# Distances and identity by outer products on the matrix engine, head-pair loads of the first batch, and a crossbar turn of the attention output

## The chip, the core and the metric

The kernel runs on one core of one Trainium2 chip. The core has a matrix engine (TensorE, PE in the profile), a vector engine (VectorE, DVE), a scalar engine (ScalarE, ACT), GpSimd (POOL), a queue engine (SyncE, SP) and 16 DMA engines. The metric is device time in microseconds (us); less is better. One run was also profiled, and all durations below are from that one.

## The reference

Local attention with eight global keys feeds a gated long convolution. There are 4 batches, 8 heads, 768 positions and 64 values per head; heads side by side make 512 channels.

```python
scores = q @ k^T / 8                      # per batch and head, 768 x 768
rel = i - j;  keep = (j < 8) | (0 <= rel < 96)
dist = where((j < 8) & not local, 96, |rel|)
a = softmax(where(keep, scores - 2**-(h+1) * dist, -1e9))
x = (a @ v) with heads side by side       # (4, 768, 512)
x1, x2, x3 = split(x @ w_proj)            # 512 channels each
y = x1 * irfft(rfft(x2, axis=1) * rfft(filter_fft, axis=0)) * x3
out = y @ w_out
```

## The kernel before

**Plan and order.** The kernel does not leave the order to a scheduler. Python code first makes a graph of about 1000 operations, each with a planned cost and the data that it reads and writes. A constant string, `ORDER`, then lists them one by one: the number of the operation, the engine that takes it (P, A, V, G or S) and, for the matrix engine, the accumulation banks. `97P1 98V` is operation 97 on PE into bank 1 and operation 98 on VectorE. Where an operation may run on ACT or on DVE (evacuations of a bank), the string chooses. Words such as `i6b1` are six filler matmuls that compute nothing. Each engine and each DMA queue works through its own part strictly in that order, so a late operand holds up all that stands behind it on the same engine.

**Attention.** Keys are cut into seven tiles. Tiles 0 to 5 start at multiples of 120; each has 8 rows for the global keys and 120 local keys. A key tile meets at most 216 query columns. Queries and keys come from HBM with positions on the partitions (`qn`, `kn`, cast to 16 bits by GpSimd's DMA queue, L322) and must be turned so that the 64 head values lie on the partitions (`QT`, `KT`). Batches 0 to 2 are turned by PE (`turned`, L652; batch 0's queries, loaded in 32 bits by SP's queue, by `turned32`, L639) and the turned bank is evacuated by ACT or DVE (L306). Batch 3 is turned by DMA transposes on SP's queue (`crossed`, L626 and L629). The three groups of key tiles (0 and 1; 2 and 3; 4 to 6) are the chunks. `scores` (L693) multiplies one pair of heads for one chunk: two heads of 64 rows each use the two halves of the array. ACT takes the exponential (L707), DVE multiplies with `mask` (L724), which holds exp(-slope * distance). For batch 0 the mask is not yet there, and PE adds the bias instead: slopes on a diagonal (`slope`) times distances (`near`), L684.

**Distances.** `distances` makes the distance tables on GpSimd (an iota and affine selects, L484 to L504), DVE patches the global rows, and six copies on ACT and DVE spread them into `near`. The identity comes from GpSimd too; 16 small scalings on ACT (L310, `eo<-ident`) make `slope`.

**Values and the turn of x.** `values` (L742, L747) multiplies the exponentials with `vn`; a column of ones gives the sum. DVE takes the reciprocal (L771) and one multiplication (L766, or several on ACT, L770) writes `xn`, with positions on the partitions. `transpose_x` turns it on PE (L787), and ACT or DVE evacuate the bank into `xT` (L306).

**Convolution.** From `xT` come the gates x1 and x3 (`gate`, L856, evacuated at L310 and L866, multiplied at L868), and through `butterfly` (DVE, L801 to L812) the operands of x2's projection (L925), the forward transform (L613), the product with the filter's spectrum, the inverse transform (L950, L953) and `half` (L1051). Product with the gates (L1056) and output projection (L977) end the batch; each 128 positions are stored by one DMA on SP's queue (L985).

Attention of batch b+1 is interleaved with the convolution of batch b.

Of the kernel before, what the change touches and what calls it, by code (L numbers as in the profile page):

```python
# [9 lines left out]
F32 = mybir.dt.float32  # L10
# [6 lines left out]
P = 128  # L17
NG = 8
KL = P - NG
HUGE = 1.0e5  # L20
MAGIC = 12582912.0
# [18 lines left out]
0V 42V 3V 7V 27S 59S 28S 60S 61S 26S 69S 4G 54A 48A 45A 56A 50A 5V 1V 6V 29G 30G 66G 33G 65G 77G i6b1 17P0 18A  # L40
58A 47A 46A 43A 19V 11V 12P1 13A 49A 44A 57A 2A 14V 8V 15V 16A 55A 53A 20V 34V 39A 21A 51A 52A 22A 36A 37A 10V
40V 35G 70G 71G 72G 32G 68G 67G 73G i15b3 120P2 121V 9V 41V 93P3 94A 97P1 98V 82V 38V 258G 31G 74G 75G 267G
266G 226P0 95P4 96A 99A 230A 100P5 i1b6 122P2 123A 87A i1b1 126P3 127V 231V 269G i2b1 124P4 125V 101V 62V 64V
229V 268G 257G 255G 256G 259G 79G 76G 78G 80G 81G 262G i2b1 128P67 129A 134P23 135A 91P1 92V 24V 63V 132P45
133A 130P67 131A 102P23 103A 168P1 169V 227V 106P45 107A 170P6 171V 232V 166P7 167A 172P1 173V 228V 25V 261S
260S 263S 264S 275G 274G 273G 272G 265G 104P23 105A 108P45 109A 176P67 177A 178P01 179A 86A 136P23 137V 138V
141P45 142V 143V 174P67 175A 83A 115P23 116V 117V 110P01 111V 112V 180P45 181A 139P6 140A 89A 88A 144P7 145V
182P23 183V 184V 118P0 119A 85A 113P1 114V 187P45 188V 189V 383P7 185P6 186A 84A 384A 385P2 386V 213V 152P3
190P4 191V 212V 219V 215V 220V 357P6 147P2 149A 358A 154A 355P5 356V 198P4 200A 90A 359P2 360V 222V 214V 488G
271G 270G 496G 487G 489S 484G 495G 485G 193P7 195A 162P3 164A 396P01 397A 398V 216V 221V 364P45 361P67 362A  # L50
365A 208P2 210A 151P3 153V 366V 223V 23V 224V 225V 217V 146P0 148A 161P1 163A 165V 150V 218V 157P4 159A 370P67
393P23 394A 395V 367P01 368A 371A 192P5 194V 369V 372V 196V 156P4 158A 160V 155V 363V 233V 234V 235V 236V 237V
238V 239V 297P2 295P3 296A 387P01 388A 298A 390P67 280P4 281A 293P3 294A 391A 207P0 299P1 308P2 309A 300A
306P3 307A 301P5 203P4 205A 302A 284P2 285A 431P1 429P3 430A 432A 202P4 204V 209V 433P5 434A 490S 504G 486G
277G 503G 501G 276G 278G 506G 502G 494G 498G 378P67 379V 380V 392V 389V 252P23 253A 254A 240P4 241V 244P1 245A
246P5 247A 248P67 250A 249A 242P0 243A 373P23 374V 375V 206V 211V 719G 282P1 435P45 436A 283A 399P67 400V 401V
251V 441P23 442A 197P0 199A 404P45 405V 310V 406V 722G 491G 493S 720S 492S 381P1 382V 376P6 377A 288P7 289A
402P2 403V 443V 286P0 287A 583P3 407P4 408A 585P5 586V 437V 290V 584V 291V 303V 438P67 439A 440V 304V 292V
444P01 587P2 588A 445A 446V 311V 715G 717S 716G 409P4 419P5 410P6 412A 421A 420P7 595P23 596A 422A 598P01 599A
425P6 424P5 426A 427A 411A 447P23 448V 305V 449V 611P7 612A 723G 497G 279G 452P01 453V 454V 728G 505G 714G  # L60
500G 659P6 660A 324P5 314P4 315A 320P7 321V 428V 600V 312P2 316P3 317A 325A 313A 450P6 661P4 662A 318P0 455P3
456V 423V 201V 451V 478V 477V 413V 597V 479V 326P5 327A 319A 322P7 415P1 417A 323A 589P23 592P45 593A 811S
414P6 416A 468P0 470A 590A 458P1 460A 613P7 614V 418V 480V 328V 329V 481V 482V 594V 330V 483V 331V 591V 332V
457P6 459A 657P0 658A 729G 507G 734G 713G 712G 499G 730G 726G 727G 725G 732G 731G 724G 735G 733G 473P2 475A
618P45 619A 620V 333V 335V 621P67 615P01 616A 622A 463P3 472P2 474A 462P4 464A 465A 512P5 513A 521P6 522A
669P01 670A 624P23 625A 626V 525P7 526A 523P6 524A 672P45 663P01 664A 508P2 509A 673A 601P67 602V 334V 603V
623V 336V 665V 617V 671V 510P3 511A 467P0 536P1 537A 666P45 667A 668V 838S 718S 814S 813S 812S 837S 882S 721S
839S 883S 340P2 341A 469A 514P1 516P3 517A 515A 632P67 604P2 534P0 535A 538V 633V 674V 527P4 528A 605A 343P3
344A 606P01 607V 634V 608V 518V 352P5 353A 354S 529P4 530A 675P23 676V 519V 471V 635P5 636A 677A 627P67 609P4
610V 680P01 681V 628V 629V 532V 682V 531V 539V 520V 533V 346P5 337P4 338A 347A 339S 345S 342S 348S 349P6 630P7  # L70
631A 821P23 824P01 825A 350A 822A 351S 678P4 679V 826V 683P5 638P7 640A 684A 705V 653P0 548P6 546P1 547A 549A
550P2 544P3 554P7 555A 551A 545A 552P4 553V 706V 708V 707V 466V 461V 709V 476V 542P1 543A 655A 686P5 688A
691P4 693A 643P2 645A 540P3 541A 556V 843P67 840P01 841A 849P45 850A 647P2 649V 637P3 639A 844A 652P0 654V
823V 557V 558V 710V 559V 842V 560V 641V 711V 701P1 703A 893P45 846P23 847A 894A 815P67 736P0 737A 816A 817V
648P1 650A 749P2 890P45 891A 750A 696P3 698A 762P0 763A 832P67 833V 563V 651V 834V 561V 848V 892V 564V 753P1
754A 642P4 644A 751P5 752A 887P23 888A 884P01 818P67 819A 820V 845V 851V 895V 656V 740P4 741A 764P5 738P2 739A
885A 765A 766V 695P3 697A 700P4 742P2 743A 827P67 828V 829V 889V 886V 562V 757P0 758A 580P5 581A 702A 744P1
685P0 687A 755P5 756A 830P4 831A 745A 857P23 858V 859A 896P67 897V 898V 901P45 902V 903A 746V 747V 760V 689V
568P0 565P1 852P67 853V 854V 759V 748V 767V 571P2 572A 577P3 578A 860P4 690P5 861V 761V 835P2 836A 566A 855P3
856A 904P6 905A 899P7 900V 927V 926V 646V 929V 928V 930V 931V 704V 932V 574P2 575A 576S 567S 573S 582S 768P1  # L80
782P4 770P6 771A 569A 570S 579S 774P3 780P2 778P7 779A 783A 769A 868P6 776P0 777A 775A 772P7 773A 781A 784V
785V 786V 699V 787V 788V 791V 862P4 950P1 951A 933P7 934A 692A 694V 789V 792V 937P0 948P1 949A 938A 946P5
935P7 936A 947A 954P1 955A 867P0 952P3 959P5 961P7 962A 869A 953A 960A 872P1 874V 957V 956V 958V 963V 964V
941P2 942A 864A 870A 917P7 939P0 940A 943V 944V 945V 802P1 803A 805P5 878P6 863P4 865A 877P0 980P1 981V 866V
790V 971P4 972A 919A 879A 880A 808P3 984P4 978P2 982P7 983A 979A 967P1 968V 985V 986V 965P0 966A 969P6 970A
973V 881V 974V 975V 987V 976V 988V 977V 1004V 989V 799P7 793P4 794A 800A 801S 795S 804S 873P6 875A 809A 876V
871V 916P2 918A 796P1 797A 991V 990V 992V 993V 994V 920V 1006V 798S 810S 921P4 912P0 914A 911P3 913A 806A 923A
807S 922P2 906P1 908A 924A 925V 915V 907P3 909A 910V 1007V 1005V 1001P0 1002A 1003S 995P1 996A 997S 998P2 999A
1000S 1008P0 1009V 1010S 1014P1 1015V 1016S 1011P3 1012A 1013S
# [108 lines left out]
class Fused:  # L198
# [11 lines left out]
    CROSS = (3,)  # L210
    LATER = ()
# [8 lines left out]
    def __init__(self, ctx, tc, q, k, v, n_global, n_local, w_proj, filt, w_out, out):  # L220
# [10 lines left out]
        self.K0 = [KL * t for t in range(6)] + [S - KL]  # L231
# [6 lines left out]
    def buffers(self):  # L238
# [5 lines left out]
        self.qn = t("qn", [P, 6, H, D])  # L244
        self.kn = t("kn", [P, 7, H, D])
        self.vn = [t(f"vn{i}", [P, 7, H, self.VD]) for i in range(2)]
        self.QT = t("QT", [P, 4, S])
# [4 lines left out]
        self.xn = [t(f"xn{i}", [P, 2, 7, 2, D]) for i in range(2)]  # L252
# [12 lines left out]
        self.h1 = t("h1", [P, 6, DM])  # L265
        self.h2 = t("h2", [P, 6, DM])
# [14 lines left out]
        self.dg = t("dg", [P, 264], BF16)  # L281
        self.far = t("far", [NG, 216])
# [7 lines left out]
        self.row = spare[0:1, 1984:2624].rearrange("p (a b) -> p a b", a=5)  # L290
        self.wide_dg = self.mix.bitcast(BF16).rearrange("p a b c -> p (a b c)")[:, 0:648]
        self.cst = t("cst", [1, 4])
        self.one = t("one", [1, P])
# [31 lines left out]
    def load_rows(self, what, dst, src, b, t):  # L325

        lo, hi = self.K0[t], self.K0[t] + KL
        self.load("G", dst[P - (hi - lo):P, t, :, 0:self.D],
                  src[b, :, lo:hi, :].rearrange("h p d -> p h d"), [what + (t,)], (8 * (hi - lo), 256),
                  f"load{what}{t}")  # L330

    def load_run(self, what, dst, src, t, n):

        rows = src[0, :, self.K0[t]:self.K0[t] + KL * n, :].rearrange("h (t p) d -> p t h d", t=n)
        self.load("G", dst[NG:P, t:t + n, :, 0:self.D], rows, [what + (i,) for i in range(t, t + n)],
                  (8 * KL * n, 256), f"load{what}{t}")

    def load_q(self, b, t):
        src = self.q[b, :, P * t:P * t + P, :].rearrange("h p d -> p h d")
        if b == 0:  # L340
            st = self.ot[t].rearrange("p (h d) -> p h d", h=self.H)
            self.load("S", st, src, [("ot", t)], (1024, 256), f"q{t}")
            if self.Q32:
                return
# [896 lines left out]
```

## Time and profile before

| what | value |
|---|---|
| median of 3 runs | 173.8 us (173.58 to 174.24) |
| the profiled execution | 173.44 us, of it a span of 171.7 us from first to last instruction |
| granted matrix clock | 0.998 |
| busy share | PE 95%, DVE 91%, ACT 88%, POOL 45% |
| HBM read and written | 25.84 MB and 6.29 MB |
| queries of batch 3 stand turned (chain of work) | 99.96 us into the span |

The page gives the busy share of each engine, then the span in 40 slices with the busy share in tenths, then the chain of work that ended last and the groups of like instructions. A group's line has the source line, engine, operation, what it writes and reads, the shape, how often, the busy time, the mean of one in ns, and the idle time ahead of it with what ended it. Matmuls are pipelined: the mean of one is its latency, and the pace is read from the chain, where pieces stand end to end.

### The profile page before, as it was taken

To read this page: it belongs to the slowest core of one execution; us is meant where nothing else is said; L and a number is where in the kernel's file an instruction comes from. 1 tells how busy PE (TensorE), PEld (TensorE's weight loads), DVE (VectorE), ACT (ScalarE), POOL (GpSimd) and SP (SyncE) were. 2 spreads that over 40 slices of the span, in tenths; PEclk is the share of its full clock that TensorE was granted. 3 is DMA by queue.
4 is the path that set the end of the run, shared out by engine and by line. 5 is a ranking of instruction groups with operands and counts; after the bars stand their busy time and mean duration, and the time that the engine had idled before them with its cause. 6 is when DMAs were issued, how large, how long until landed. Compare 5 with 4: busy or idle time off the path is not lost.

```text
span 171.7 us, 4390 instructions
## 1 busy us (share of the span) xinstructions
PE 162.3 (95%) x1675; PEld 102.2 (60%) x1675; DVE 156.7 (91%) x355; ACT 151.1 (88%) x309; POOL 77.4 (45%) x95
## 2 busy tenths in 40 slices
PE   6888899999999979999999999999999999999990
PEld 1365689865464757965455767654576745575540
DVE  7997989989999899999999998999989999999960
ACT  5799999999899979999999999999998986866841
POOL 8999999962499994948993000000000000000000
PEclk9999999999999999999999999999999999999999
DMA  6999999999999999999999996500000360000854
GB/s 127 181 207 151 144 154 146 169 203 187 148 151 142 144 144 135 87 140 137 156 151 134 153 188 199 230 4 0 0 4 0 117 256 0 0 0 28 308 217 186
DMA packets 98077, 22.44 MB, mean 131 GB/s; under 512 B 90808, under 2 KB 94984, under 8 KB 98056
## 3 DMA queue, kind: packets, MB, share of 16 engines
q0 software_dynamic: 80912, 12.14, 100.3%
q1 hardware_dynamic: 17144, 10.02, 22.2%
q8 instruction: 13, 0.21, 0.5%
q14 instruction: 8, 0.07, 0.1%
HBM read 25.84 MB, written 6.29 MB: 187 GB/s over the span
## 4 chain that ended last, share of the span: by engine, by line
PE 72%; DMA 6%; POOL 6%; DVE 6%; ACT 6%; issue 2%; ACTq 0%; DVEq 0%
PE bank L856 23%; PE bank L925 9%; PE bank L977 9%; PE bank L950 5%; PE bank L693 5%; PE bank L613 5%; PE bank L652 4%; DMA QT<-qn 3%; PE bank L787 3%; PE bank L742 3%; DMA qn<-in_q_dram 3%; POOL kn L322 3%; PE bank L747 3%; POOL vn L322 2%; PE bank L684 2%
## 5 line engine op out<-in xcount | busy, mean ns | idle before, releaser
L856 PE MATMUL bank<-xT,w 128*128 128x384 f16 x256 | 47.4, 326 | 0.0
L707 ACT ACTIVATE E<-bank 128x864 f16<-128x864 f32 x48 | 41.4, 917 | 0.7 <-ACT h L310 0.3
L856 PEld LDWEIGHTS <-w 128*128 128x128 f16 x256 | 23.8, 98 | 16.3 <-issue 1.1
L322 POOL DMA_DIRECT2D vn<-in_v_dram x28 | 25.7, 923 | 4.4 <-DMA g<-in_moe_filter_fft_dram 3.9
L322 POOL DMA_DIRECT2D kn<-in_k_dram x28 | 25.9, 934 | 2.7 <-PE bank L856 2.2
L977 PE MATMUL bank<-wo,y 128*128 128x512 f16 x96 | 22.8, 379 | 0.0
L724 DVE TENSOR_TENSOR E<-E,mask 128x864 f16<-128x864 f16 x36 | 20.8, 603 | 0.8 <-ACT E L707 0.8
L322 POOL DMA_DIRECT2D qn<-in_q_dram x18 | 16.3, 917 | 6.1 <-PE bank L652 5.6
L310 ACT ACTIVATE ot<-bank 128x512 f32<-128x512 f32 x22 | 13.3, 618 | 4.6 <-PE bank L977 4.0
L866 ACT CAST g<-bank 128x384 f16<-128x384 f32 x32 | 15.9, 536 | 1.1 <-PE bank L856 0.9
L310 ACT ACTIVATE ab<-bank 128x512 f16<-128x512 f32 x24 | 14.2, 619 | 2.6 <-PE bank L925 2.5
L766 DVE TENSOR_TENSOR xn<-bank,rc 128x512 f16<-128x512 f32 (+1 forms) x21 | 16.0, 764 | 0.5
L742 PE MATMUL bank<-vn,E 128*128 128x65 f16 x224 | 15.3, 193 | 0.0
L742 PEld LDWEIGHTS <-E 128*128 128x128 f16 x224 | 14.0, 97 | 1.9
L747 PE MATMUL bank<-vn,E 128*128 128x65 f16 x192 | 15.1, 193 | 0.0
L977 PEld LDWEIGHTS <-y 128*128 128x128 f16 x96 | 8.9, 98 | 9.3 <-DVE y L1056 0.2
L693 PE MATMUL bank<-QT,KT 64*128 64x216 f16 (+2 forms) x224 | 13.9, 241 | 0.3 <-DMA QT<-qn 0.3
L306 ACT CAST X<-bank 128x512 f16<-128x512 f32 x24 | 13.6, 610 | 0.6 <-PE bank L613 0.5
L310 ACT ACTIVATE x<-bank 128x384 f16<-128x384 f32 x25 | 12.5, 526 | 1.3 <-DVE g L868 1.0
L747 PEld LDWEIGHTS <-E 128*128 128x128 f16 x192 | 13.2, 97 | 0.5
L306 ACT CAST eo<-bank 128x384 f16<-128x384 f32 x27 | 11.5, 508 | 1.4 <-PE bank L953 1.4
L693 PEld LDWEIGHTS <-KT 64*128 64x128 f16 x224 | 8.5, 94 | 6.3 <-issue 4.4
(142 smaller groups left out, 354.8 us busy)
## 6 DMA issues: line engine op xcount, KB each, us to landing
out_dram<-ot SPq DMA_DIRECT2D x24, 256.0 KB
kn<-in_k_dram POOLq DMA_DIRECT2D x28, 120.0 KB, 5.4
vn<-in_v_dram POOLq DMA_DIRECT2D x28, 120.0 KB, 5.2
qn<-in_q_dram POOLq DMA_DIRECT2D x18, 128.0 KB, 5.3
ot<-in_q_dram SPq DMA_DIRECT2D x6, 256.0 KB
w<-in_moe_w_proj_dram POOLq DMA_DIRECT2D x4, 256.0 KB, 6.7
g<-in_moe_filter_fft_dram POOLq DMA_DIRECT2D x1, 768.0 KB, 14.1
w<-in_moe_w_proj_dram POOLq DMA_DIRECT2D x1, 512.0 KB, 9.4
```

What stands on the lines that cost most here:

```text
L306: {"A": nc.scalar.copy, "V": nc.vector.tensor_copy, "G": nc.gpsimd.tensor_copy}[e](out, in_)
L310: self.nc.scalar.mul(out, in_, c)
L322: return self.g.op(eng, 0.57 + 0.00035 * nbytes[0] if eng == "G" else 0.5, lambda _: e.dma_start(dst, src), w=w, r=r, nbytes=nbytes, name= ...
L693: nc.tensor.matmul(bs[hh].f32()[:, off:off + w], self.KT[hs, m, hp], self.QT[hs, hp, KL * m:KL * m + w], start=(off == 0 and not near), st ...
L707: g.op("A", act(864), lambda _: nc.scalar.activation(eo, bs[0].two()[:, :, 0:432].rearrange("p h (m w) -> p h m w", m=2), Act.Exp, scale=s ...
L724: g.op("V", dve(864, 2), lambda _: nc.vector.tensor_mul(eo, eo, mk), r=[("mask", 2 * hp), ("mask", 2 * hp + 1)], w=[("E", hp, gi)], name=" ...
L742: nc.tensor.matmul(o[:, n, hh], ef[:, at:at + P], vt[:, t, 2 * hp + hh, 0:D + 1], start=first, stop=(t == 0), skip_group_check=True)
L747: nc.tensor.matmul(o[:, n, hh], ef[:, at:at + P], vt[:, t - 1, 2 * hp + hh, 0:D + 1], start=False, stop=True, skip_group_check=True)
L766: nc.vector.tensor_mul(to, o[:, :, :, 0:D], rc.to_broadcast([P, 2, 2 * nt, D]))
L856: nc.tensor.matmul(bk.f32()[:, 0:h], self.w[:, c, o + P * j:o + P * j + P], self.xT[:, c, h * s:h * s + h], start=(c == 0), stop=(c == 3))
L866: g.op("A", act(h), lambda _: nc.scalar.copy(x3, pts[1].f32()[:, 0:h]), use=[pts[1]], w=[ko], name="x3")
L977: nc.tensor.matmul(bk.f32(), y[:, c, P * t:P * t + P], self.wo[:, c, :], start=(c == 0), stop=(c == 3))
```

## The change

1. **Distances and identity** are made on PE by outer products of counting rows (`dist`), then turned into tables by two absolute values on ACT and some small DVE instructions. GpSimd makes no table any more. Eight slope scalings replace 16, and any may run on DVE.
2. **Batch 0** loads q and k per head pair, in token order (positions (6 x 128) instead of overlapping tiles), by eight DMAs of 1536 rows on GpSimd's queue; SP loads no queries. PE turns each pair with 12 transposes of 64 columns (`six`), and one evacuation (a 720 and a 48 column copy) cuts the tiles.
3. **Queries of all batches** lie in seven tiles of 120 positions (before: six of 128), so `QT` has the layout of `KT`. A score matmul of 216 or 168 columns becomes two (120 and 96, or 120 and 48).
4. **Batch 3's** q and k are turned by two DMA transposes each (before: six and three).
5. **x of batches 1 to 3** is turned by 21 DMA transposes on SP's queue, one for each tile (`crossed_x`), in place of `transpose_x` and its evacuation. `xn` is one tile with heads side by side, so a DVE scaling becomes two.
6. **The last 128 rows** of the output are projected, evacuated and stored in two halves of 256 columns.
7. Smaller memsets (only what is read of `vn`'s ones), a smaller h1/h2, and a new `ORDER` with 22 filler matmuls (before: 27).

```diff
@@ distances
-        def first(_):
-            for ap, w, base in ((dg[:, 0:n], n, NG), (dg[:, n:n + 48], 48, NG + o)):
-                p.iota(ap, pattern=[[-1, w]], base=-base, channel_multiplier=1,
...
+        def dist(_):
+            one, neg, n2, mm = self.one, self.neg, self.n2, nc.tensor.matmul
+            for k, bk in enumerate(bks):
+                o, w = bk.f32(), 384 if k == 0 else 264
+                mm(o[:, 0:w], neg, one[:, 0:1].to_broadcast([1, w]), start=True, stop=False, skip_group_check=True)
+                mm(o[:, 0:n], one, n2[:, NG:NG + n], start=False, stop=(k == 0), skip_group_check=True)
...
+                v.tensor_scalar(ident[lo:lo + 64, lo:lo + 64], d[lo:lo + 64], 0.0, None, op0=Alu.is_equal)
...
+                tt, bks[k].f32()[:, 0:w], Act.Abs, bias=self.mid, scale=HUGE2), use=[bks[k]], r=["mid", "ident"] if k == 0 else ["mid"],
...
@@ loads of batch 0
+    def load_six(self, what, dst, src, i):
+        self.load("G", dst[:, i], src[0, 2 * i:2 * i + 2].rearrange("h (t p) d -> p (h t) d", p=P),
+                  [(what + "six", i)], (1536, 256), f"six{what}{i}")
...
+    def six(self, what, i):
...
+            for r in range(6):
+                for hh in range(2):
+                    nc.tensor.transpose(b.f16()[64 * hh:64 * hh + 64, P * r:P * r + P], buf[:, r, hh], self.ident)
...
@@ scores
-                    nc.tensor.matmul(bs[hh].f32()[:, off:off + w],
-                                     self.KT[hs, m, hp],
-                                     self.QT[hs, hp, KL * m:KL * m + w],
...
+                for x in range(1 + (w > KL)):
+                    n = w - KL if x else min(w, KL)
+                    for hh in range(2):
+                        nc.tensor.matmul(bs[hh].f32()[:, off + KL * x:off + KL * x + n], self.KT[hs, m, hp],
+                                         self.QT[hs, m + x, hp, 0:n], start=(off == 0 and x == 0 and not near),
...
@@ the turn of x
+    def crossed_x(self, c):
+        for t in self.GRP[c]:
+            at, n = KL * t - 8 * (t % 2), (P if t % 2 else P - 16) if t < 6 else 48
+            self.g.op("S", 1.25, lambda _, at=at, n=n, t=t: self.nc.sync.dma_start(
+                self.xT[:, :, at:at + n], self.xn[0:n, t].rearrange("p h d -> p (h d)"), transpose=True),
...
             for j in range(2):
                 self.values(j, c, b % 2)
-                self.transpose_x(j, c)
+                if b not in self.XX:
+                    self.transpose_x(j, c)
+            if b in self.XX:
+                self.crossed_x(c)
...
@@ output
+            for lo, hi in ((0, 256), (256, 512)) if last and t == 5 and self.HALVES else ((0, 512),):
```

## The prediction

> **What bounds the kernel now.** I read the page's engine row and slices first, then three windows, then the chain.
>
> ```profile
> PE 162.3 (95%) x1675; PEld 102.2 (60%) x1675; DVE 156.7 (91%) x355; ACT 151.1 (88%) x309; POOL 77.4 (45%) x95
> DMA  6999999999999999999999996500000360000854
> PE 72%; DMA 6%; POOL 6%; DVE 6%; ACT 6%; issue 2%; ACTq 0%; DVEq 0%
> ```
> ```profile
> 0.00:20.00 20.00, 16.04 (x138) 9.34 (x139) 16.61 (x58) 16.97 (x41) 18.77 (x30) 1.00 1.60 163
> 20.00:160.00 140.00, 138.48 (x1501) 89.18 (x1500) 133.92 (x282) 128.36 (x258) 58.64 (x66) 1.00 1.23 119
> 160.00:171.70 11.70, 7.79 (x41) 3.72 (x38) 6.18 (x17) 5.73 (x13) 0.00 (x0) 0.98 0.57 219
> ```
> The columns of the windows are start:end, length, then PE, weight loads, DVE, ACT and POOL. From 20 to 160 us PE has work for 138.5 of 140 us: it is the bound, so a matmul less is time less. But DVE is close behind, idle for only 140 - 133.92 = 6.1 us; ACT has 11.6 us. In the first 20 us PE's 16 us hold much filler, and the chain runs over DVE and ACT:
>
> ```profile
> 3.88 0.84 DVE eo L385 x4
> 4.90 1.12 DVE kn L397
> 9.98 0.68 ACT eo L306 x2
> 13.42 0.96 ACT QT L306 x2
> 16.85 0.74 ACT mask L543
> 17.60 1.57 ACT E L707 x2
> 21.25 0.45 PE bank L639 x4
> 28.81 0.45 PE bank L787 x8
> 35.99 0.67 PE bank L693 x12
> 88.82 5.37 DMA qn<-in_q_dram
> 94.19 5.77 DMA QT<-qn
> 117.83 0.67 PE bank L693 x16
> ```
> The pace of PE is read here: 0.45/8 = 56 ns for a 16-bit turn (L787; L652 stands in the chain at the same 0.45 for 8), 112 ns for a 32-bit turn (L639). Batch 3's queries take 11 us from their issue to PE, through a load and a transpose.
>
> **PE, part by part.**
> *x turned elsewhere.* 112 turns become 28: 84 x 56 ns = -4.7 us, all on the path. PE's wait for `xn` ahead of them (1.0 us, row L787 below) loses its place too; I count it at nothing, since the next values wait for the same DVE.
> *Scores in two pieces.* 224 matmuls become 416. The two heads of a pair run side by side, and the columns stay the same. The two L693 rows show what pieces cost: 12 matmuls of 216 columns took 0.67 us, and 16 of mixed widths (216, 168, 48) with the same total of columns took 0.67 us too. Bounds: 0, and 0.03 us for each of 96 extra pairs (the pace of a 65 column values matmul, pieces of 0.06 for two in the chain) = 2.9 us. I take +0.4, near the row of the same instruction.
> *q and k of batches 1 and 2.* 48 query turns become 56: 8 x 56 ns = +0.45 us.
> *Batch 0.* 24 x 112 + 28 x 56 ns = 4.3 us go; 96 turns with half the columns of the array come. Bounds: 28 ns each if two lie side by side (2.7 us) and 56 ns if not (5.4 us). I take 35 ns, 3.4 us, because the score rows show halves side by side: -0.9 us (-1.6 to +1.1). The 8 distance matmuls (some 1560 columns, about 0.7 us) and 5 fillers less lie in the start, where PE waits anyway.
> After the start this leaves -4.7 + 0.4 + 0.45 = -3.9 us (-4.7 to -0.9).
>
> **ACT and DVE.**
> ```profile
> L787 PE MATMUL bank<-ident,xn 128*128 128x128 f16 x112 | 9.1, 219 | 1.0 <-DVE xn L766 1.0
> L306 ACT COPY xT<-bank 128x480 f16<-128x480 f16 x10 | 5.9, 585 | 2.1 <-PE bank L787 2.1
> L306 DVE COPY xT<-bank 128x480 f16<-128x480 f16 x6 | 2.3, 400 | 0.0
> L766 DVE TENSOR_TENSOR xn<-bank,rc 128x512 f16<-128x512 f32 x15 | 10.2, 687 | 0.3
> L310 ACT ACTIVATE eo<-ident 64x64 bf16<-64x64 f16 x16 | 3.4, 248 | 0.1
> ```
> ACT: 13 evacuations of xT become 3 (-8 x 0.585 - 2 x 0.696 = -6.1 us); 16 slope scalings and 6 table copies (3.4 + 2.3) give way to 5 scalings and 2 absolute values (about 2.2): -3.5; 12 more small xn scalings at 0.21 each +2.5; four more x1 evacuations +2.1; fewer of ab, X and ot -4; the rest +1.4. Sum -7.6 us.
> DVE: 11 evacuations of xT become 3 (-3.4); 21 xn scalings become 32 of about half the size (17 pieces replaced by 26 at 0.42 to 0.55): +0.8; x1 evacuations -2.2; ab, X and ot taken over from ACT +4.5; smaller memsets of vn and kn -3.4; tables and batch 0's evacuations about +2; the rest -0.5. Sum -2.2 us, of it some -0.7 ahead of the first reciprocal and -1.5 behind. So DVE gains least: if PE's 140 us shrink by 3.9, DVE has to do 132.4 us of work in 136.1, 97.3% instead of 95.7%. I give back 1.0 us for that (0 to 3).
>
> **The start.** The first exponential starts at 17.50 us. Ahead of it ACT loses 16 scalings (3.4), table copies (2.3), three QT casts (1.6), the twin, KT and inr copies (1.4) and a mask (0.7), 9.4 us; it gains two absolute values (0.9), three scalings (0.75), a copy of v's first rows (0.6), an evacuation each of k and q (2 x 1.0) and a small copy (0.2), 4.5 us: -4.9. DVE's counting row drops from seven dependent doublings (2.1 us) to two instructions. What may be late in its place is the load: POOL takes 0.92 us for 960 rows, so 1.47 for 1536 (an estimate); the third load, the first pair's second half, is issued by 0.7 + 3 x 1.47 = 5.1 us and lands 5.4 us later (page, kn), at 10.5. Turn, evacuation, sines (1.0) and a table load (1.3) put the first exponential at 14 to 14.6, some 3 us earlier. The last queries are the tenth load in the queue (issued by 14.3, landed by 20) and needed for the ninth exponential, at about 21. POOL pays 12288 rows instead of 6720, +5.3 us, and loses its table work (4.34 to 8.52 us and 0.6), so v, w and batch 1's loads behind them stand where they stood. I take -2.5 us (0 to -4.9); batch 0's PE gain lies in it.
>
> **The end.** The last evacuation shrinks from 0.60 to about 0.40: -0.2 us.
>
> **SP and DMA.** 21 turns at the measured issue of 1.5 us (row below) are 32 us of a queue that has the room. Behind them stand stores and the copies of global rows; ahead of batch 2's first turn stand batch 3's first KT and QT transposes, which wait for loads.
> ```profile
> L629 SPq DMA_TRANSPOSE QT<-qn x6: 1192/1515/2042, 88.9 to 103.5; - x6
> ```
> That is an answer on the tile QT: least, median and greatest ns of an issue. A chunk's last three turns take 3 x 1.5 + 5.8 = 10.3 us from `xn` to the butterfly. Between them the new order lays DVE work of about 9.3, 10.3 and 7.5 us (batches 1 to 3, products at 0.69, masks at 0.60, g at 0.35). Batch 3 is short by 2.8; but its transposes find no loads in the way, and the 5.8 was taken while loads ran, so I count nothing.
>
> The skill weighs against this part. The Trainium skill, VectorE: DVE Perf Modes, "The three transpose paths", gives a 128 x 128 turn 390 ns on TensorE and 1309 ns through the crossbar, and its rules for kernel authors send such turns to TensorE when PSUM will do. No row here times one block alone. By that figure, as an estimate, three tiles (12 blocks) would take 15.7 us, 20 us more than the three covers together, and the kernel would be near 188 us.
>
> **Sum.** -2.5 - 3.9 + 1.0 - 0.2 = -5.6 us on the profiled execution's 173.44, 167.9; that run lies 0.36 us under the median of 173.8. I forecast 168.0 us. Its own range, with the bounds above, is 165.5 to 170.
>
> **Rivals.**
> *DVE binds* (0.18). The idle share of DVE stays as it is and the new order has no better fit. Then only 1.5 us behind the start, 1 us in it and 0.2 at the end are won: 170.7 us. For: 95.7% busy. Against: in the windows from 140 to 160 us it already ran at 97%.
> *Turns late* (0.12). At the greatest issue, 3 x 2.04 + 5.77 = 11.9 us, the three covers are short by 2.6, 1.6 and 4.4; at the median by 1.0, 0 and 2.8. DVE stands at the butterfly, masks and reciprocals queue behind it, and PE follows. That takes 3.8 to 8.6 us off the gain; near the lower end 172.5.
> *Batch 3's loads late* (0.12), the slower side. The DMA row reads 9 until slice 24. The 14 turns of batches 1 and 2 add 7168 rows of 256 B; at the mean pace of small packets (90808 in 103 us, 880 per us) that is 8.1 us if there is no room. Batch 3's queries would stand turned at 100 - 2.5 + 8.1 = 105.6, and behind that point PE saves only 28 turns (1.6) and the end: 173.44 + 5.6 - 1.8 = 177.2 us. It decides from about 4 us of lateness on. Against: a DMA engine counts as busy while a packet is under way, POOL waits longest for buffers that PE holds (5.6 us, L652), and its waits from 36 to 81 us come to 12.8 us, over a quarter of that stretch.
> *All bounds good* (0.03): 163.5 us.
>
> **Chances.** Forecast 0.55. About 0.5% can be told from no change here. Faster: 0.55 + 0.18 + 0.03 and a third of the late turns, 0.80; same, most of the other late turns, 0.08; slower 0.12. The range leaves out the late loads and the outermost late turns above, and the best case below: 164 to 173.5.
>
> **What would show it.** Right: first exponential near 14 us; L787 with 28 turns and L693 with 416 at unchanged busy time for a chunk; DVE over 93% of a span of 166. Wrong: PE waiting for `DMA xT` or DVE waiting for `DMA xT` at the butterfly (late turns); a wait for `DMA QT` or `DMA KT` of several us before batch 3's scores (late loads); PE idle behind DVE in every stage (DVE binds); L693's pieces at over 30 ns a pair more (split not free).

## The result and the profile after

The changed kernel took 179.56 us (median of 4 runs, 178.28 to 181.23), the kernel before 173.69 beside it: 1.0346 times as long (95% interval 1.0291 to 1.0401). Forecast were 168.0 us and a range of 164.0 to 173.5. The profiled execution took 179.99 us with a span of 178.2. Medians below are over all runs, while ratios and their intervals leave out every run more than 1.5% above the fastest of its kernel (two of four in e4), so the two can differ by a per cent, and the profiles of e1, e4, e5, e10 and e17 are of runs left out.

The page of the changed kernel, in the rows that were shown of before:

```profile
PE 165.5 (93%) x1842; PEld 101.4 (57%) x1842; DVE 153.8 (86%) x383; ACT 145.0 (81%) x297; POOL 74.7 (42%) x89
...
DMA  6999999999999999999999999927103220404446
...
PE 67%; DMA 15%; DVE 7%; POOL 6%; issue 2%; SPq 1%; ACT 1%; DVEq 0%
```

DVE and ACT have less to do, as forecast (156.7 to 153.8 and 151.1 to 145.0 us). But the DMA share of the chain rose from 6% to 15%, and the DMA engines stay at 9 through slice 26 instead of 24. The windows (start:end, length, then PE, weight loads, DVE, ACT, POOL, granted clock, DMA share, GB/s):

```profile
0.00:20.00 20.00, 18.77 (x195) 9.65 (x197) 13.94 (x71) 11.88 (x25) 14.34 (x19) 1.00 1.63 105
20.00:160.00 140.00, 131.99 (x1559) 83.10 (x1555) 127.34 (x281) 121.82 (x250) 60.38 (x71) 0.99 1.38 129
160.00:178.20 18.20, 14.70 (x98) 8.61 (x94) 12.55 (x35) 11.27 (x24) 0.00 (x0) 0.98 0.49 187
```

From 20 to 160 us PE now lacks 8.0 us of work, 6.5 more than before. The chain, from three stretches, shows where (start, length, what):

```profile
7.96 1.82 PE bank L314 x4
9.78 0.78 PE bank L682 x10
10.55 1.39 PE bank L314 x3
...
64.43 6.63 DMA kn<-in_k_dram
71.10 0.62 PE bank L707 x8
...
99.35 8.73 DMA xT<-xn
108.08 0.05 issue
108.13 0.82 PE bank L930 x4
```

Three places answer to the forecast's steps. At the start the turns of batch 0 (L682) stand behind filler matmuls (L314). At 71 us PE takes up batch 2's keys as soon as their load lands, 6.6 us after its issue. At 108 us the first gate of batch 2 (L930) stands at a crossbar turn of x. PE's waits for DMAs in this kernel (total, times, longest):

```profile
PE bank L751 <- DMA QT<-qn: 2.9, 1, 2.9
...
PE bank L930 <- DMA xT<-xn: 2.2, 1, 2.2
...
PE bank L707 <- DMA kn<-in_k_dram: 0.7, 1, 0.7
```

The groups that the change meant to shrink did shrink (112 turns of x to 28, 24 evacuations to 6, three of them on ACT; the scalings of the three batches are smaller and more). Line, engine, what, count, busy, mean ns:

```profile
L832 DVE TENSOR_TENSOR xn<-bank,rc 128x256 f16<-128x256 f32 (+1 forms) x26 | 10.9, 464 | 0.1
...
L853 PE MATMUL bank<-ident,xn 128*128 128x128 f16 x28 | 2.0, 219 | 0.0
```

and the turns that take their place are, one by one, cheaper than priced. From the answer on the tile xT (least, median, greatest; ns of SP's queue for the issue, then us to landing):

```profile
L863 SPq DMA_TRANSPOSE xT<-xn x21: 1177/1262/2435, 58.8 to 139.2; - x21
...
DMA to landing us min/median/max: 2.3/5.1/8.3
```

Priced were 1.5 and 5.8. So the question was where 12 us went although the median turn was no dearer than its price.

### The profile page after: what moved, and what is told of

The parts are those of the page before. It is cut to its first block, busy times and chain, and to the rows that moved or that the text cites. A ratio compares the mean times of both kernels' runs of the same rounds, so it can differ in the third digit from the quotient of the medians.

```text
span 178.2 us, 4734 instructions
## 1 busy us (share of the span) xinstructions
PE 165.5 (93%) x1842; PEld 101.4 (57%) x1842; DVE 153.8 (86%) x383; ACT 145.0 (81%) x297; POOL 74.7 (42%) x89
## 4 chain that ended last, share of the span: by engine, by line
PE 67%; DMA 15%; DVE 7%; POOL 6%; issue 2%; SPq 1%; ACT 1%; DVEq 0%
PE bank L930 20%; PE bank L1065 11%; PE bank L1010 8%; DMA g<-in_moe_filter_fft_dram 6%; PE bank L314 5%; DMA xT<-xn 5%; PE bank L635 4%; PE bank L1035 4%; DMA kn<-in_k_dram 4%; PE bank L751 4%; PE bank L801 2%; POOL vn L334 2%; PE bank L707 2%; PE bank L806 2%; POOL kn L334 2%
## 5 line engine op out<-in xcount | busy, mean ns | idle before, releaser
L930 PE MATMUL bank<-xT,w 128*128 128x384 f16 x256 | 48.8, 332 | 3.1 <-DMA xT<-xn 2.2
L930 PEld LDWEIGHTS <-w 128*128 128x128 f16 x256 | 24.1, 99 | 20.5 <-DMA xT<-xn 2.7
L334 POOL DMA_DIRECT2D qn<-in_q_dram x25 | 23.0, 923 | 12.9 <-PE bank L707 6.9
L334 POOL DMA_DIRECT2D kn<-in_k_dram x25 | 22.5, 906 | 6.2 <-PE bank L682 3.1
L1065 PE MATMUL bank<-wo,y 128*128 128x512 f16 (+1 forms) x100 | 23.3, 371 | 0.0
L751 PE MATMUL bank<-QT,KT 64*128 64x120 f16 (+2 forms) x416 | 15.3, 204 | 3.4 <-DMA QT<-qn 2.9
L751 PEld LDWEIGHTS <-KT 64*128 64x128 f16 x416 | 11.3, 94 | 10.6 <-issue 8.4
L322 ACT ACTIVATE x<-bank 128x384 f16<-128x384 f32 x29 | 14.4, 525 | 0.7 <-PE bank L930 0.5
L801 PE MATMUL bank<-vn,E 128*128 128x65 f16 x224 | 14.8, 193 | 0.0
L322 ACT ACTIVATE ot<-bank 128x512 f32<-128x512 f32 (+1 forms) x20 | 12.1, 609 | 3.4 <-PE bank L1065 2.4
L806 PE MATMUL bank<-vn,E 128*128 128x65 f16 x192 | 14.6, 193 | 0.0
L635 PE MATMUL bank<-ab,fwd 128*128 128x512 f16 x40 | 11.8, 379 | 0.1
```

The costliest lines, as they stand in the source:

```text
L322: self.nc.scalar.mul(out, in_, c)
L334: return self.g.op(eng, 0.57 + 0.00035 * nbytes[0] if eng == "G" else 0.5, lambda _: e.dma_start(dst, src), w=w, r=r, nbytes=nbytes, name= ...
L635: self.nc.tensor.matmul(b.f32(), self.fwd[:, f], src(i, t), start=(n == 0), stop=(n == len(terms) - 1))
L751: nc.tensor.matmul(bs[hh].f32()[:, off + KL * x:off + KL * x + n], self.KT[hs, m, hp], self.QT[hs, m + x, hp, 0:n], start=(off == 0 and x ...
L801: nc.tensor.matmul(o[:, n, hh], ef[:, at:at + P], vt[:, t, 2 * hp + hh, 0:D + 1], start=first, stop=(t == 0), skip_group_check=True)
L806: nc.tensor.matmul(o[:, n, hh], ef[:, at:at + P], vt[:, t - 1, 2 * hp + hh, 0:D + 1], start=False, stop=True, skip_group_check=True)
```

## Experiments: turning x elsewhere, and the queue

Theories, in the names of the expectations: Q, batch 2's turns stand on SP's queue behind batch 3's transposes; C (later G), the turns slow what runs beside them; S, the start; P, the new order or batch 0's loads; T, the crossbar turns in whatever way; W, waits that other work could cover.

**Batch 3's transposes behind batch 2's turns.**
```diff
- ... 328S 691S 783S 785S 329P1 ...  654S 655S 653S 784S 786S
+ ... 328S 691S 329P1 ...            654S 655S 653S 783S 785S 784S 786S
```


> The changed kernel took 179.6 us, 11.6 more than forecast. Edit: on SP's queue the first KT and the first QT transpose of batch 3 are issued behind the last x turn of batch 2 instead of ahead of its first; nothing else moves. Theory Q (queue): batch 2's x turns stand behind these two (1.4 and 5.0 us of issue) and land late, which costs PE 5.1 us of waiting from 90 to 110 us and about 2 us by the clock that drops behind it; then batch 2's first gates start near 101 us instead of 108 and the time is 173 to 176 us. Theory C (contention): every crossbar turn slows all rows that the DMA engines move, whatever its order; then batch 3's queries and keys now come late instead, and the time is 178 to 182 us. Theory S (start): the loss is the missing gain at the start; 179 to 180 us.

188.23 us, 1.07 (1.0584 to 1.0815) against before. PE's first scores of batch 3 now wait:

```profile
PE bank L751 <- DMA QT<-qn: 11.2, 1, 11.2
```

All three expectations missed. The order of the queue was the better one already: with batch 3's transposes second PE stands 11.2 us at them, where it stood 2.9 us at them and 2.2 us at the turn before.

**x on PE for batch 2, and for all batches.**
```diff
-    XX = (1, 2, 3)
+    XX = (1, 3)          # e2;   XX = ()  in e3, each turn and evacuation behind its scaling in ORDER
```


> Edit: batch 2's x is turned on PE and evacuated as before the change; its seven crossbar turns go; batches 1 and 3 keep theirs. It costs PE 28 turns, 1.6 us, and ACT and DVE three evacuations each. Theory Q: the stall from 98 to 108 us and the clock drop go, 173 to 175 us. Theory C: a third of the turns go, and with them a third of the loss, 176 to 178 us. Theory S: 180 to 181 us.

> Edit: x of all batches is turned on PE, as before the change; no crossbar turn of x is left, the rest of the change stays. By the forecast's own prices this kernel should lose 4.7 us of PE's gain and keep the start's 2.5 and the end's 0.2, so 171.5 to 172.5 us. Theories Q and C: 171 to 174 us, since both put the loss on the turns. Theory S: the start brings nothing and the x turns cost nothing, so 179 to 184 us.

179.38 (ratio 1.0315) and 191.38 (1.0924): both misses, and neither is a price of the turn. PE stood at the scalings, which the turns on PE need first, 5.2 us in e2 (three waits ahead of L853) and longer in e3:

```profile
PE bank L853 <- ACT xn L836: 6.7, 3, 3.1
PE bank L853 <- DVE xn L826: 2.3, 4, 1.5
```

Two more such versions, with the turns further back, did not mend it.
```diff
-    XX = (1, 2, 3)
+    XX = (3,)            # turns 1.5 to 2.6 us of PE work behind the scalings (e7); scalings all on DVE (e12)
```


> Edit: x of batches 1 and 2 is turned on PE again, with each group of turns put behind 1.5 to 2.6 us of other PE work after its scaling, so that PE does not stand at it (the kernels that turned x on PE before this one put it right behind and lost several us there); batch 3's seven turns stay on the crossbar, where no loads run. PE gets 56 turns more, 3.1 us. Theory T: 172 to 175 us. Theory P: 179 to 182 us.

> A version that might win. Edit: x of batches 1 and 2 on PE (56 turns, 3.1 us), its scalings all on DVE (0.69 us in one instruction instead of up to 2.46 us in 12 on ACT, behind which PE stood in the last such kernel), the evacuations on ACT; batch 3's x on the crossbar. Theory T: no crossbar turn of x is left beside the loads, 171 to 175 us. If PE turns placed into this order still make PE wait, 176 to 181 us.

183.73 (1.0553) and 182.55 (1.0563). Both missed their ranges. PE still waits at single places, and query buffers are freed late; in e7 POOL's loads of queries show it:

```profile
POOL qn L334 <- PE bank L707: 15.9, 2, 13.1
```

These four show only that this order has no room for turns on PE; a new order for them was not made.

**The turns alone in the kernel before.**
```diff
-                self.transpose_x(j, c)
+            if b in self.XX:            # (1, 2, 3); before's ORDER, crossx behind the two scalings
+                self.crossed_x(c)
```


> The kernel before, in its own order, its own start and its own scores, with this one part of the change: x of batches 1 to 3 is turned by 21 crossbar DMAs, each issued on SP behind the two scalings that it needs; PE's 84 turns and 18 evacuations go, and the scalings of DVE come in two halves. Theory T: the turns cost more than PE's 4.7 us, 176 to 182 us. Theory P: PE gains without the new order's loss, 169 to 172 us.

211.25 us, 1.2074 (1.195 to 1.2198), far above both ranges. The gates of before's order follow the scalings closely, and PE stands at the turns in four waits (gate is L875 here):

```profile
PE bank L875 <- DMA xT<-xn: 31.1, 4, 10.4
```

The new order hides most of that: 2.2 us of waiting for `xT` are left in the changed kernel.

## Experiments: what of a turn costs the time

**8-row copies, and plain copies of the same bytes, at the turns' places.**
```diff
-                self.xT[:, :, at:at + n], self.xn[0:n, t].rearrange("p h d -> p (h d)"), transpose=True),
+                self.xT[0:8, 0, at:at + n], self.xn[0:8, t].rearrange("p h d -> p (h d)")[:, 0:n]),   # e5
+                self.xT[0:n, :, at:at + n], ...rearrange("p (a c) -> p a c", a=4)[:, :, 0:n]),        # e6
```


> Edit: each of the 21 crossbar turns of x becomes a plain copy of 8 rows of 96 to 256 B into xT, at the same place of SP's queue and with the same waits; the turning of x is left out, and nobody does it. So PE, DVE and ACT have the work of the changed kernel without the turns' issue time, landing and traffic. Theory T (the turns, by SP's issue time of 26 us between 86 and 115 us and by their landing): the stalls of PE near 70 to 80 and 90 to 110 us go, 168 to 172 us. Theory P (the new order, or batch 0's 128-byte loads): the turns are not what is late, 176 to 180 us.

> Edit: each of the 21 crossbar turns becomes a plain DMA of the same bytes (4 pieces of up to 256 B for each of up to 128 partitions), so x is copied and not turned. Theory T by the crossbar (issue and landing of a transposing DMA): a plain copy issues in 0.7 us instead of 1.2 to 2.5, the stalls shrink, and the time lies near that of the 8-row copies, 169 to 173 us. Theory T by traffic (7168 more rows in the stretch in which the loads run): the rows are still there, 176 to 180 us.

The 8-row copies gave 170.3 to 175.4 us in four runs, too wide for an interval, with a median of 174.64 between its two ranges. The plain copies gave 173.37 us in ten, 0.9992 (0.995 to 1.0035) of before, just above the range for the crossbar's theory and below that for the rows'. So 21 DMAs of the same bytes, with the same waits, at the same places, cost 6 us less than 21 transposing ones: it is the transposing, not the rows. The shorter issue on SP's queue comes with the plain copy and was not tried apart from it. The issue halves, the median landing hardly changes:

```profile
L863 SPq DMA_DIRECT2D xT<-xn x21: 607/655/2167, 56.0 to 131.0; - x21
...
DMA to landing us min/median/max: 2.3/4.8/9.8
```

**Only batch 2's, only batch 1's turns as plain copies.**
```diff
-            self.g.op("S", 1.25, lambda _, at=at, n=n, t=t: self.nc.sync.dma_start(
+            self.g.op("S", 1.25, lambda _, at=at, n=n, t=t, plain=self.b in (2,): ...   # the copy of e6 if plain; (1,) in e18
```


> Edit: only batch 2's seven turns of x become plain DMAs of the same bytes (batch 2's x is copied, not turned); batches 1 and 3 keep theirs. All three plain gave 173.4, none 179.6. Crowding (batch 2's turns, batch 3's transposes and loads together from 86 to 115 us): 4 to 6 us go, 173.5 to 175.5 us. Each turn alike: a third goes, 177 to 178.5 us.

> Edit: only batch 1's seven turns become plain DMAs (batch 1's x is copied, not turned). Crowding: only the stall near 70 to 80 us goes (batch 2's keys land 6.6 us after their issue there, PE idle 1.6), 177.5 to 179 us. Each turn alike: 177 to 178.5 us, and as much as batch 2's.

176.29 (1.0157, 1.0076 to 1.0238) and 176.72 (1.0204, 1.0124 to 1.0284): the first lies between its two ranges, the second just under both. Batch 2's turns cost 3.3 us and batch 1's 2.5 by the ratios (1.0346 less these, of 174), each uncertain by more than a microsecond; together they come near the 6. Batch 3's turns were not tried alone. The windows tell the two apart (PE is the second column after the times). First the changed kernel, then batch 2 plain, then batch 1 plain:

```profile
60.00:80.00 20.00, 17.91 (x268) 12.75 (x264) 17.95 (x42) 18.29 (x39) 13.35 (x16) 1.00 2.33 141
...
90.00:120.00 30.00, 24.90 (x263) 15.38 (x260) 22.48 (x53) 22.18 (x60) 5.83 (x7) 0.94 1.52 139
```
```profile
60.00:80.00 20.00, 17.47 (x268) 12.77 (x266) 17.51 (x42) 17.85 (x39) 12.78 (x15) 1.00 2.19 139
...
90.00:120.00 30.00, 26.85 (x300) 16.65 (x298) 24.72 (x57) 24.07 (x65) 6.33 (x8) 0.94 1.58 145
```
```profile
60.00:80.00 20.00, 19.46 (x287) 13.62 (x284) 19.58 (x46) 19.81 (x42) 14.98 (x18) 1.00 1.78 139
...
90.00:120.00 30.00, 24.45 (x255) 14.79 (x252) 22.44 (x50) 21.70 (x54) 3.36 (x4) 0.94 1.42 154
```

Batch 1's turns make PE's 2.1 us of idling from 60 to 80 us (0.5 without them), batch 2's make 2 us of the 5.1 from 90 to 120. The other kernels bear it out, whatever their start: from 60 to 80 us PE idles 1.9 to 3.2 us in the ten with batch 1's turns on the crossbar, 0.1 to 0.5 in the five with copies at their places (e5, e6, e9, e16, e18); from 90 to 120 us 4.6 to 11.3 us in nine with batch 2's turns, 1.3 to 3.2 in five with copies. The granted clock does not tell the three kernels apart (0.94 from 90 to 120 us in each).

What batch 2's turns do there is a plain wait: with them copied, PE's 2.2 us at `xT` are gone, and the wait for batch 3's queries, 2.9 us above, stays:

```profile
PE bank L751 <- DMA QT<-qn: 3.2, 1, 3.2
```

How batch 1's do it is in the DMA view of 56 to 76 us, the changed kernel first, then batch 1 plain (queue: packets, MB, time of the packets as a share of 16 engines; then a load with its median us to landing):

```profile
GB/s 151 162 158 165 145 150 151 151 158 226 199 57 42 104 146 154 155 170 155 143 152 217 152 114 147 222 43 11 51 141 150 144 155 149 155 141 152 149 151 152
...
q0 software_dynamic: 18551, 2.25, 217.3%
...
kn<-in_k_dram POOLq DMA_DIRECT2D x6, 120.0 KB, 6.4
```
```profile
GB/s 153 147 146 159 148 130 95 131 146 137 162 159 157 147 153 149 146 160 191 204 176 225 161 153 144 152 148 151 154 148 150 153 158 177 183 144 140 59 221 178
...
q0 software_dynamic: 18732, 2.22, 177.9%
...
kn<-in_k_dram POOLq DMA_DIRECT2D x6, 120.0 KB, 5.4
```

About as many load packets take 23% longer each (217.3% of 16 engines' 20 us for 18551 packets, 37.5 ns each, against 177.9% for 18732, 30.4 ns), and the median load of keys lands a microsecond later. PE meets that at 71 us. Every kernel of the new order says the same: from 56 to 76 us it is 33 to 45 ns in the ten with batch 1's turns on the crossbar, and 30.4 to 30.6 ns in the eight without (plain copies, 8-row copies or turns on PE). The traffic also falls to 42 and to 11 GB/s (slices of 0.5 us), the second time while the load of keys in the chain is under way; but single slices fall low without crossbar turns too (59 here, 26 in e6), so this alone shows nothing.

**Batch 3's q and k as plain copies, with and without x's.**
```diff
-            g.op("S", 1.25, lambda _, dst=dst, src=src: sync.dma_start(dst, src, transpose=True), ...
+            g.op("S", 1.25, lambda _, dst=dst, src=src: sync.dma_start(dst, src), ...   # src as 128-column blocks
```


> Edit: only the four transposes of batch 3's queries and keys become plain DMAs of the same bytes (q and k of batch 3 are not turned); the 21 turns of x stay on the crossbar. Theory Q (in line on SP: x's turns stand behind the merged transposes' 5.0 and 6.7 us of issue): the stall near 98 to 108 us goes, 172 to 175 us, near that of plain x turns. If the x turns' own landing is what is late, the stall stays: 177 to 180 us.

> Edit: besides the 21 turns of x, the four transposes of batch 3's queries and keys become plain DMAs of the same bytes too, at the same places; x of batches 1 to 3 and batch 3's q and k are copied and not turned, nobody turns them. With only the x turns plain the time was 173.4 us, and 12.0 us passed there between the issue of the three-tile QT transpose and its landing, with 2.9 us of PE waiting for it and a clock of 0.86 behind. Theory T, carried on: the rest of the forecast's gain is lost in this one transpose; without it 167.5 to 170 us. Rival (the new order or the loads take the rest): 172 to 174 us.

177.86 (1.0278) with x on the crossbar, 172.02 (0.9915, 0.9871 to 0.9958) with nothing on it. The second lies in its rival's range and not in theory T's: batch 3's transposes are not where most of the rest was lost. The first is what was expected if x's turns land late by themselves. Theory Q falls once more: with batch 3's transposes gone PE waits for x itself, 4.6 us instead of 2.2.

```profile
PE bank L930 <- DMA xT<-xn: 4.6, 1, 4.6
```

**Smaller transposes for batch 3.**
```diff
-    QX = ((0, 3), (3, 7));  KX = ((0, 2), (2, 7))
+    QX = ((0, 1), (1, 2), (2, 3), (3, 5), (5, 7));  KX = ((0, 2), (2, 4), (4, 7))
```


> Edit: batch 3's queries are turned in five transposes (tiles 0, 1, 2, 3-4, 5-6) instead of two (0-2, 3-6), its keys in three (0-1, 2-3, 4-6) instead of two (0-1, 2-6), at the same places of SP's queue. If merging is what makes a transpose land late (12.0 us for 12 blocks, 5.8 us for one of 4 blocks in the kernel before), the scores of batch 3 start some 3 us earlier: 176 to 178 us. If issue and landing go by the blocks, the same: 179 to 181 us.

181.3 us, 1.0449 (1.0348 to 1.055): no gain, so splitting does not help.

**More work ahead of the waits.**
```diff
- ... 503P4 504A 619P5 505P1 506A ... 676V 610P0 ... 614P4 520P1 ...
+ ... 503P4 504A 505P1 506A ... 520P1 516P2 528P3 799P67 524P1 518P4 802P23 530P0 526P1 522P4 ... 619P5 610P0 614P4 ... 676V   # e13
- 512P1 513A 787P23 788A 796P67 797A 486P0 487A 510P1 511V ... 499P4 500A 501P5 502A
+ 512P1 513A 486P0 487A 510P1 511V 499P4 500A 501P5 502A ... 787P23 788A 796P67 797A                                           # e14, besides
```


> Edit to the order alone: batch 1's eight inverse groups (2.6 us of PE) with their mixing on DVE, and the first values of batch 3 (0.8 us), are put ahead of batch 2's eight first gates, and batch 2's butterfly behind batch 1's mixing; the turns stay as they are. Theory W (an uncovered wait): PE's 2.2 us at batch 2's first gate and DVE's wait at the butterfly go, and a part of the clock drop: 175 to 177.5 us. Theory G (the turns slow everything beside them): 178.5 to 181 us.

> As the kernel with batch 1's inverses ahead of batch 2's first gates, and besides three projections and a spectrum of batch 1 (3 us of PE) ahead of batch 3's first scores, which stood 2.9 us at the first QT transpose. Theory W: both waits are covered and the clock stays up, 173 to 176 us. Theory G: 178 to 181 us.

179.93 (1.0412) and 181.53 (1.0459): theory W fails, G is nearer. In e14 the scores of batch 3 no longer come too early for their queries, but these land 13.3 us after their issue, and the chain goes through them:

```profile
87.17 13.29 DMA QT<-qn
...
100.51 0.38 PE bank L751 x8
```

## Experiments: the start

```diff
- ... 56G i9b2 5P01 ... 37V i4b4 77P1 234G 49G i3b4 89P0 90A i3b5 87P4 ... 38A i3b2 79P0
+ ... 56G i3b2 5P01 ... 37V 77P1 234G 49G 89P0 90A 87P4 ... 38A 79P0      # e4; on top of e14 in e15, of e9 in e16
```


> Edit: of the 22 filler matmuls ahead of the first scores 19 go (nine become three, and 4, 3, 3 and 3 become none). Theory S: the turns of batch 0 wait for the fillers (9.2 us of PE in the first 15.6), not for the loads; without them the first exponential starts near 13 to 14.5 us instead of 17.6, and the time falls by 2 to 4 us, to 175.5 to 178. If the loads are what is late, the first exponential stays at 17 to 17.6 and PE's clock at the first scores may be lower: 179.5 to 181 us. Theories Q and C: an earlier start only meets the stall near 100 us earlier or waits for the same loads: 178 to 180 us.

> The last kernel with 19 of the 22 fillers left out as well: a version that might win. The two edits add if they mend different waits: theory W and theory S, 171 to 174 us; if the earlier start only meets the loads earlier, as the last one, 173 to 176 us.

> All 25 transposing DMAs as plain copies (x of batches 1 to 3 and batch 3's q, k are not turned) and 19 of 22 fillers left out. Without the fillers' edit it was 172.0 us, its first exponential at 16.1 us. Theory S: the rest of the forecast's gain is in the start, 168 to 170.5 us, near the forecast's 168.0. If engine work (PE's 143.5 us behind the start, 3.9 less forecast than before, 2.8 measured) is what is missing: 171.5 to 172.5 us.

177.44 us (1.0129, 1.008 to 1.0178), as theory S expected; 2.1% less than the changed kernel by the ratios, 1.2% by the medians, and the fastest with its arithmetic whole, behind the one before. 178.77 (1.0352) with the work laid ahead, outside both of its ranges; 170.53 (0.9869, 0.9834 to 0.9904) with all 25 transposes as plain copies, between its two. PE's start, first in the changed kernel, then in e2, whose start is the same code, then with three fillers:

```profile
1.19 4.02 PE L314 MATMUL bank<-idle 128*128 128x512 f16 x9 [1.19 <-DVE few L385]
...
7.89 1.89 PE L314 MATMUL bank<-idle 128*128 128x512 f16 x4
9.71 0.85 PE L682 MATMUL bank<-ident,qn 128*64 128x128 f16 x12
10.49 1.46 PE L314 MATMUL bank<-idle 128*128 128x512 f16 x3
```
```profile
1.19 3.59 PE L314 MATMUL bank<-idle 128*128 128x512 f16 x9 [1.19 <-DVE idle L378]
...
6.20 1.04 PE L314 MATMUL bank<-idle 128*128 128x512 f16 x4
7.16 0.53 PE L682 MATMUL bank<-ident,qn 128*64 128x128 f16 x12
7.62 0.82 PE L314 MATMUL bank<-idle 128*128 128x512 f16 x3
```
```profile
1.19 1.46 PE L314 MATMUL bank<-idle 128*128 128x512 f16 x3 [1.19 <-DVE idle L378]
...
5.96 0.85 PE L682 MATMUL bank<-ident,qn 128*64 128x128 f16 x12 [0.33 <-DVE warm L379]
```

The first turn starts at 9.71, 7.16 or 5.96 us, the first exponential at 17.62, 15.05 or 14.48. So the loads were there; the fillers were ahead in PE's queue, and the same fillers take longer in some executions than in others: one more costs 0.43 us in the changed kernel (1.89 less 1.46), 0.22 in e2 (1.04 less 0.82), half and full pace. Of the fifteen profiles with these 22 fillers, four kept the half pace until some 13 us or later (first exponential at 17.2 to 17.7); eleven were at full pace by 7 us (15.05 to 16.1). So much of what the profile of the changed kernel shows at the start is its execution. In the kernel of plain copies, where less is late, the edit is worth 0.5% (0.9915 to 0.9869).

## Why the forecast was wrong

The forecast's 0.967 (168.0/173.8) and the measured 1.0346 lie 6.8% apart, 11.8 us. Going back from the changed kernel: plain x copies take off 3.5% (6.1 us), plain q and k copies 0.8% (1.3 us), fewer fillers 0.5% (0.8 us). Then 2.0% (3.5 us) are left. So the turns of x are the whole of why the kernel became slower, but only half of why the forecast was missed: with plain copies in their places the time is that of the kernel before (0.9992) and not 168. In the profile of the last kernel PE still waits 2.2 us for `xT`, plain as the copies are:

```profile
PE bank L930 <- DMA xT<-xn: 2.2, 1, 2.2
```

That wait and the missing part of PE's gain (below) are both large enough to be most of the 3.5; they were not separated, and this part stays open.

- **SP and DMA, "so I count nothing": the step that failed.** It should have stood at +6 us for x's turns. I compared one chunk's issue and landing (1.5 and 5.8 us a turn, medians 1.26 and 5.1 measured) with DVE's work ahead of the butterfly. Two things were left out. The first to wait was PE, at batch 2's first gate, which needs only the first two chunks: it stood 2.2 us at a turn that landed 8.7 us after its issue, and with batch 2's turns copied that wait was gone (3.3 us by the ratio). And batch 1's turns made the loads beside them slower (37.5 ns a packet against 30.4), at which PE idled 1.5 us more from 60 to 80 us (2.5 us by the ratio). The windows thus show 3.5 of the 6 us; how the rest comes about is not shown. Batch 3's transposes cost some 1 us more than counted at most: the kernel before has such transposes too, and PE waited 0.3 us for them there, 2.9 here.
- **The start, -2.5.** The loads came in time, and 14 to 14.6 us for the first exponential was in reach (14.48). The failing sentence is that the distances and fillers "lie in the start, where PE waits anyway": PE was busy for 18.77 of the first 20 us, and its fillers stood ahead of real turns. The Trainium skill, TensorE: Matmul & The Clock Gate, "What's actually happening", describes a half-rate clock that goes full after a busy window of some 3.4 us whose phase differs by run. The fillers agree on half and full pace (0.43 and 0.22 us for one more) and on a moment that differs by run; but in the changed kernel the pace stayed low until 13.9 us with PE busy from 1.2 on, far longer than that page says.
- **PE's work, -3.9 after the start: under half of it came.** PE's busy time without its fillers fell from 154.2 us (162.3 less 8.1) to 152.6 (160.1 less 7.5) in the kernel with 25 plain copies, both at a granted clock of 1.00: some -1.7 us, where -3.9, -0.9 for batch 0 and +0.7 for the distances were forecast. The split of the scores was sized too low: L693's 13.9 us of busy time became 15.3 in L751, +1.4 and not +0.4. Where the rest is was not found. Its range, -4.7 to -0.9, is also not the sum of its bounds, which give -4.25 to -1.35. The rows, of before and of the kernel with 25 plain copies:

```profile
L302 PE MATMUL bank<-idle 128*128 128x512 f16 x27 | 8.1, 435 | 1.2 <-DVE idle L375 1.2
```
```profile
PE 160.1 (95%) x1842; PEld 99.8 (59%) x1842; DVE 154.3 (91%) x383; ACT 144.1 (85%) x297; POOL 74.4 (44%) x89
...
L314 PE MATMUL bank<-idle 128*128 128x512 f16 x22 | 7.5, 483 | 1.8 <-DVE few L385 1.2 <-DVE eo L536 0.6
```

- **DVE and ACT:** -2.9 and -6.1 us measured, -2.2 and -7.6 forecast. That DVE would bind was not seen: in the kernel without transposes PE has 138.0 of 140 us from 20 to 160 and DVE 134.3.
- **The end, -0.2:** not tried by itself.
- **Rivals.** The turns late (172.5) had a right place and the wrong waiter: PE at the gate, not DVE at the butterfly; the turns' effect on loads was not in it. Batch 3's loads late (177.2, given 0.12) came nearest in time, partly by luck. PE did wait for batch 3's queries, 2.9 us, but the price was wrong in kind: 7168 more rows were to take 8.1 us if there was no room, and plain copies of these rows cost nothing that can be told (0.9992). There was room for the rows and none for turning them. The rule of the Trainium skill that the prediction weighed (VectorE: DVE Perf Modes, "Rules for kernel authors") pointed the right way; that page's figure, taken for each block and added up, gave 188 us, 8 too many (a turn of four blocks took 1.18 us to issue and 2.3 to land at the least, 5.1 at the median).

No kernel that computes the whole reference was faster than the one before.

## What to carry to other kernels

Before work goes from a bound engine to a DMA transpose, look what else the DMA engines carry in that stretch and who is the first to wait, for the turn or for a load beside it: here both were paid for, and the median time of one turn showed neither. A plain copy of the same bytes in the same place separates the turning from the bytes in one run. Filler matmuls are work like any other for what stands behind them in PE's queue. A busy time that is compared from a fixed moment on counts work that only moved ahead of that moment as saved.

## What the runs showed of the hardware

- Crossbar transposes on one queue slow the packets of another: 33 to 45 ns for a load packet in ten kernels (56 to 76 us, seven turns or part of them in that stretch), 30.4 to 30.6 ns in eight without, those with plain DMAs of the same bytes among them.
- A transposing DMA holds SP's queue for 1.26 us (median) where the plain one of the same bytes takes 0.66; the median landing is nearly the same (5.1 and 4.8).
- PE's pace in the first 14 us is half or full by execution, with a granted clock of 1.00 in both; it moves the first exponential by up to 2.6 us.
- While PE stood for long and just behind, the granted clock fell: to 0.69 from 110 to 120 us in e1, whose wait was 11.2 us, and to 0.86 in the changed kernel behind its shorter ones; in windows of 2 us the least is 0.50 in both.
